# Up projection of the last four blocks by eleven half-width products in place of six full-width ones, with its sums spread over VectorE and GpSimd

## The chip, the cores and the metric

The kernel runs on one core of a Trainium2 chip. The metric is the device time of one execution in microseconds; the profile shows one execution, and the times are of executions of their own.

## The reference, cut to what matters

Two stages in float32. The first is a delta-rule attention with a state of 48 x 48 for each of 4 x 8 heads, over 768 positions; the second is an MLP with a hard-swish between its two products, over 3072 tokens (d_model 384, d_ff 2048).

```python
for t in range(S):                       # k_n: normalised keys
    y[:, :, t] = einsum('bhd,bhde->bhe', q[:, :, t], state)
    v_old = einsum('bhde,bhd->bhe', state, kt)
    state = state + bt[:, :, :, None] * einsum('bhd,bhe->bhde', kt, vt - v_old)
x = y.transpose(0, 2, 1, 3).reshape(B * S, H * D)          # 3072 x 384
h = x @ w_in                                               # w_in 384 x 2048
g = h * clip(h + 3.0, 0.0, 6.0) / 6.0
out = g @ w_out                                            # w_out 2048 x 384
```

## The kernel before, in words

**Tokens.** A token tile is 32 positions of all four batches, 128 rows; there are 24 (t = 0 to 23). Two token tiles make a block of the MLP (256 tokens, 12 blocks). Token tiles are also grouped for the attention's triangular inverse: group 0 is tile 0, then groups of four (1 to 4, 5 to 8, ... 17 to 20), the last, group 6, of three (21 to 23).

**Attention.** `prep(t)` normalises keys and scales them on GpSimd (L479, L457 the masks `mb`, L467 `bkb`), transposes keys and queries on TensorE (L495), copies them out with ScalarE (L503, the buffers `KQ`) and forms the score matrices (L516, evicted by VectorE at L527). `norms(g)` squares the keys (L385 on ScalarE in groups 0 to 3, L387 on GpSimd from group 4 on), reduces (L391) and takes roots. `inverse(g)` inverts the triangular matrices of a group by substitution on VectorE, 30 steps of a product (L728) and a difference (L733), with a transposition before and after (L447, L451). `chain(t)` carries the state: its products with keys and queries (`ks`, L775), R on VectorE (L788), the product with the inverse (`pz`, L796; Z on ScalarE, L882), the state's update (`su`, L893, L908), the output (`py`, L796; L812, L788, L831) and, last, the transposes `yt` (L841) that ScalarE copies into the block's `xT` (L845).

**MLP.** `up(blk)` forms, for each of 16 chunks of 128 hidden units, three matmuls of 256 columns (the three slices of d_model; L947) into a PSUM tile `ph`; ScalarE takes the relu (L955), VectorE the minimum and the product (L958) into the tiles `g`, two chunks in each. `down` (L987) is used for blocks 0 and 1. From block 2 on `down_by_seven` does the down projection by seven products of half size (Strassen-Winograd): its sums of `g` are in place on VectorE (L1038), its products have 192 columns (L1052), ScalarE copies them out (L1059), VectorE adds them up (L1062), and SP writes them to DRAM. In float32 every matmul stands in the trace as two records, each with its weight load (PEld).

**Order.** The program is scheduled by hand: each engine's queue holds its instructions in the order in which the code issues them. The text `ORDER` issues everything up to the start of token tile 5, word by word. From then on a loop takes each token tile in 15 steps, u = 0 to 14. At a step it issues, in this order: the step's entry in `plan` (pieces of `chain` and `prep`), key loads, one unit of the MLP (`take(units)`: one chunk of `up`, or half a product of `down_by_seven`), and two or three pieces of `fill` (the norms, then the substitution, of a coming group). `plan` puts the state products at u = 0, R at 1, y at 3, `pz` at 4, `su` and `py` at 8, the state's sum and y's at 9, and the transposes into `xT` at 11. A block's 16 units of `up` and 14 of `down_by_seven` make 30 units, two token tiles: `up` of block 8 starts at u = 12 of tile 17 and ends at u = 12 of tile 18, and so on; that of block 11 begins at u = 12 of tile 23 and has no attention beside it for the most part.

PSUM tiles `pt`, `ph`, `po`, `pz`, `py`, `yt` share four buffers. `needs(...)` only asserts at build time that something was issued before; real waits come from the reads and writes of the buffers.

Of the kernel before, what the change touches and what calls it, by code (L numbers as in the profile page):

```python
# [9 lines left out]
FP32 = mybir.dt.float32  # L10
# [28 lines left out]
k*2 v h4 i2*2 u rb i2 gb n9 i2 u i2 v i2 ru i2 gu i2 u ru i2*3 v q gu i2 c n9 u k i2 u i2 u ru gu  # L39
q ru i2 gu i2 k n9 v i2 u h4 y4 i2 v*2 i2 n9 u y4 i2 q u*2 i2 u n9 ru i2*3 q k gu q*2 i2 n9 q i2*3  # L40
n9 u k n9 q e i2*4 ru u gu y4 h4 e n9 u y4 k n9 k*2 i2 k*5 i2*2 k*3 ru k ru gu i2 u gu p9 u e i2 u
i2*5 e u i2*4
# [4 lines left out]
def kernel(  # L47
# [65 lines left out]
    NKB, NQB, NBKB, NLB, NKQ = 2, 4, 8, 8, 7  # L113
    kbufs = [persist.tile([P, H, DP], FP32, name=f"kb{i}") for i in range(NKB)]
    qbufs = [persist.tile([P, H, DP], FP32, name=f"qb{i}") for i in range(NQB)]
    bkbufs = [persist.tile([P, H, DP], FP32, name=f"bkb{i}") for i in range(NBKB)]
# [46 lines left out]
    NVF = 3  # L163
# [213 lines left out]
    def norms(g, i0, n):  # L377

        kf = kfs[g]
        ss = small.tile([P, n, H], FP32, name="ss")  # L380
        for i in range(n):
            needs(("k", first(g) + i0 + i))
            sq = work.tile([P, H, D], FP32, name="sq", bufs=1)
            if g < 4:
                nc.scalar.activation(out=sq[:], in_=kf[:, i0 + i], func=ACTF.Square)  # L385
            else:
                nc.gpsimd.tensor_tensor(  # L387
                    out=sq[:], in0=kf[:, i0 + i], in1=kf[:, i0 + i], op=ALU.mult
                )
            yield 1  # L390
            nc.vector.tensor_reduce(out=ss[:, i, :], in_=sq[:], axis=AX.X, op=ALU.add)  # L391
            yield

        root = small.tile([P, n, H], FP32, name="root")
        nc.scalar.activation(out=root[:], in_=ss[:], func=ACTF.Sqrt, bias=tiny, scale=0.25)
        yield
        t = small.tile([P, n, H], FP32, name="nt")
        nc.vector.reciprocal(out=t[:], in_=root[:])
        yield
        nc.vector.scalar_tensor_tensor(  # L400
            out=t[:], in0=ss[:], scalar=0.25, in1=t[:], op0=ALU.mult, op1=ALU.mult
        )
        yield
        nc.vector.scalar_tensor_tensor(
            out=t[:], in0=t[:], scalar=1e-6, in1=root[:], op0=ALU.add, op1=ALU.add
        )
        yield
        inv = small.tile([P, n, H], FP32, name="inv", bufs=4)
        nc.vector.reciprocal(out=inv[:], in_=t[:])
        for i in range(n):  # L410
            invs[first(g) + i0 + i] = inv[:, i, :]
        yield
# [40 lines left out]
    def mask(t):  # L453
        mb = mbs[t] = work.tile([P, 2, NP, 2, C], FP32, name="mb")
        needs("beta")
        for e in range(2):
            nc.gpsimd.tensor_tensor(  # L457
                out=mb[:, e],
                in0=beta_tok[:, t, e:H:2].unsqueeze(2).unsqueeze(3).to_broadcast([P, NP, 2, C]),
                in1=mask2[:].unsqueeze(1).to_broadcast([P, NP, 2, C]),  # L460
                op=ALU.mult,
            )
        yield

    def scaled(t):
        needs(("kb", t), *pad(t), *([("bkb", t - NKB)] if t >= NKB else []))
        nc.gpsimd.tensor_tensor(  # L467
            out=bkbufs[t % NBKB][:, :, 0:D], in0=kbufs[t % NKB][:, :, 0:D],
# [69 lines left out]
    def product(t):  # L538
# [10 lines left out]
        ring("KQ", NKQ, ("x", t))  # L549
        VYTF = work.tile([P, 4, H * C], FP32, name="VY", tag="KQ", bufs=NKQ)  # L550
# [84 lines left out]
    def join(t):  # L635
# [7 lines left out]
        ring("KQ", NKQ, ("x", t))  # L643
        tiles = work.tile([P, 4, H, C], FP32, name="VY", tag="KQ", bufs=NKQ)
# [111 lines left out]
    def chain(t, whole=True):  # L756
# [8 lines left out]
        bkb = bkbufs[t % NBKB]  # L765
# [96 lines left out]
        else:  # L862
            needs("parity")
            Rt = work.tile([P, DM], FP32, name="R", bufs=1)
# [16 lines left out]
        Zt = work.tile([P, DM], FP32, name="Z", bufs=1)  # L881
# [20 lines left out]
        su = update() if t < N - 1 else []  # L902
        if whole:
            take(outs[t])
# [15 lines left out]

    gs, pos, evicts = {}, {}, []
# [13 lines left out]
    def up(blk, half_of=None):  # L935
# [5 lines left out]
        for f in range(NFC):  # L941
# [28 lines left out]
            yield  # L970

# [60 lines left out]
    def down_by_seven(blk):  # L1032
# [31 lines left out]
        settle()  # L1064
        product(4, A22, T4, 0)
        yield
        product(4, A22, T4, 1)
        copy(C21, 4, -1.0)
        yield
        product(2, A12, B21, 0)  # L1070
        yield
        product(2, A12, B21, 1)
        copy(C11, 2)
        sums(ALU.add, A22, A21, A22, lo)
        yield
        product(1, A11, B11, 0)
        sums(ALU.add, A22, A21, A22, hi)
        yield
        product(1, A11, B11, 1)
        copy(u, 1)  # L1080
# [36 lines left out]
    def mlp_units():  # L1117
# [3 lines left out]
        for f in range(0, NFC, WF):  # L1121
# [3 lines left out]
            for _ in range(WF):  # L1125
                next(u1)
                yield
        for blk in range(1, N // CB):
            if blk < FIRST:
                for c in range(CB):  # L1130
                    for f in range(0, NFC, WF):
                        if c == 0:
                            needs(*(("read", ("ph", blk, f + i, None)) for i in range(2)))
                        down(blk, c, f)
                        yield
            else:
                yield from down_by_seven(blk)
            if blk + 1 < N // CB:
                for n, _ in enumerate(up(blk + 1)):
# [21 lines left out]
    LA = 6  # L1161
    LE = 4
    LS = G0 + GS
# [85 lines left out]
    with tc.manual_schedule():  # L1249
# [12 lines left out]
        for t in range(LS, N):  # L1262
# [11 lines left out]
            if i == 2:  # L1274
# [11 lines left out]
                11: lambda: take(ch),  # L1286
                13: lambda: take(later),
# [6 lines left out]
            for u in range(NU):  # L1294
# [15 lines left out]
                take(fill, 2 + (u % 3 == 0))  # L1310
# [33 lines left out]
```

## Time and profile before

| What | us |
|---|---|
| median of 3 executions | 689.24 (689.07 to 690.17) |
| the profiled execution's own time | 688.24 |
| its span, from the first to the last instruction | 686.5 |
| TensorE (PE) matmul busy | 647.2 |
| VectorE (DVE) busy | 467.8 |
| ScalarE (ACT) busy | 238.9 |
| GpSimd (POOL) busy | 95.2 |
| granted TensorE clock, mean | 0.985 |

Rows of a group or of a timeline give: start, duration, engine, line, operation, what is written and read, shape, count, and in brackets the engine's idle time just before and what ended it. Matmuls are pipelined, so the duration of one (273 ns or more) is longer than its distance to the next; the distance is what a stream costs.

### The profile page before, as it was taken

To read this page: it belongs to the slowest core of one execution; us is meant where nothing else is said; L and a number is where in the kernel's file an instruction comes from. 1 tells how busy PE (TensorE), PEld (TensorE's weight loads), DVE (VectorE), ACT (ScalarE), POOL (GpSimd) and SP (SyncE) were. 2 spreads that over 40 slices of the span, in tenths; PEclk is the share of its full clock that TensorE was granted. 3 is DMA by queue.
4 is the path that set the end of the run, shared out by engine and by line. 5 is a ranking of instruction groups with operands and counts; after the bars stand their busy time and mean duration, and the time that the engine had idled before them with its cause. 6 is when DMAs were issued, how large, how long until landed. Compare 5 with 4: busy or idle time off the path is not lost.

```text
span 686.5 us, 25308 instructions
## 1 busy us (share of the span) xinstructions
PE 647.2 (94%) x11208; PEld 567.8 (83%) x11208; DVE 467.8 (68%) x1210; ACT 238.9 (35%) x476; POOL 95.2 (14%) x147
## 2 busy tenths in 40 slices
PE   2668989999999999999999999999999999999997
PEld 2458877776688988988988988988988989989997
DVE  5898776888746997846985745985546985445242
ACT  5995677421233232232232232232232132132220
POOL 6241022203521100400101302100000000000000
PEclk9977899999999999999999999999999999999999
DMA  7987125412041030031030030020020020000000
GB/s 197 246 199 189 37 66 139 82 24 47 15 79 30 2 68 6 2 78 29 3 64 9 3 71 2 2 61 1 3 48 2 2 48 2 25 3 1 25 0 24
DMA packets 88494, 33.20 MB, mean 48 GB/s; under 512 B 80160, under 2 KB 83232, under 8 KB 88384
## 3 DMA queue, kind: packets, MB, share of 16 engines
q1 hardware_dynamic: 88128, 31.29, 20.5%
q8 instruction: 88, 1.44, 0.9%
q10 hardware_dynamic: 256, 0.30, 0.2%
q14 instruction: 22, 0.18, 0.1%
HBM read 26.84 MB, written 4.72 MB: 46 GB/s over the span
## 4 chain that ended last, share of the span: by engine, by line
PE 73%; DVE 12%; DMA 7%; issue 3%; ACT 2%; SPq 1%; POOL 0%; DVEq 0%; ACTq 0%; POOLq 0%
PE ph L947 33%; PE po L1052 21%; PE po L987 4%; PE ks L775 3%; PE py L796 2%; PE su L893 2%; PE pz L796 2%; DVE g L1038 2%; DMA w_out<-in_moe_w_in_dram 2%; DVE pr L728 2%; DVE A L733 2%; PE sc L516 2%; PE pt L495 2%; DMA spare<-in_moe_w_in_dram 2%; DMA qb<-in_q_dram 1%
## 5 line engine op out<-in xcount | busy, mean ns | idle before, releaser
L947 PE MATMUL ph<-xT,w_in 128*128 128x256 f32 (+1 forms) x1248 | 271.3, 371 | 3.8 <-DVE g L958 2.3
L947 PEld LDWEIGHTS ph<-xT,w_in 128*128 128x128 f32 x1248 | 222.3, 194 | 33.1 <-DVE g L958 3.5
L955 ACT ACTIVATE g<-ph,halves 128x256 f32<-128x256 f32 (+1 forms) x208 | 94.4, 456 | 198.1 <-PE ph L947 196.5
L958 DVE SCALAR_TENSOR_TENSOR g<-g,ph 128x256 f32<-128x256 f32 (+1 forms) x208 | 81.7, 396 | 100.1 <-ACT g L955 99.9
L1052 PE MATMUL po<-w_out,g 128*128 128x192 f32 x640 | 113.3, 328 | 0.0
L1052 PEld LDWEIGHTS po<-w_out,g 128*128 128x128 f32 x640 | 103.9, 190 | 0.5
L1052 PE MATMUL po<-spare,g 128*128 128x192 f32 x480 | 84.8, 330 | 0.0
L1052 PEld LDWEIGHTS po<-spare,g 128*128 128x128 f32 x480 | 78.1, 190 | 1.8
L1038 DVE TENSOR_TENSOR g<-g 128x256 f32<-128x256 f32 x160 | 65.5, 463 | 0.5 <-PE po L1052 0.4
L733 DVE TENSOR_TENSOR A<-A,pr 128x30 f32<-128x30 f32 (+9 forms) x150 | 52.2, 348 | 3.4
L728 DVE TENSOR_TENSOR pr<-A 128x30 f32<-128x30 f32 (+9 forms) x150 | 51.1, 341 | 3.1
L334 ACT ACTIVATE spare<-spare,places 128x768 uint16<-128x768 uint16 (+1 forms) x56 | 52.4, 940 | 1.9 <-DMA spare<-in_moe_w_in_dram 1.0
L987 PE MATMUL po<-w_out,g 128*128 128x384 f32 x128 | 45.6, 493 | 0.0
L479 POOL TENSOR_TENSOR kb<-kf,inv 128x384 f32<-128x384 f32 x24 | 23.0, 958 | 155.2 <-PE pt L495 69.9
L457 POOL TENSOR_TENSOR mb<-beta_tok,mask 128x256 f32<-128x256 f32 x48 | 34.9, 748 | 66.6 <-DVE LB L527 66.5
L1059 ACT ACTIVATE o<-po 128x192 f32<-128x192 f32 x40 | 13.2, 330 | 88.1 <-PE po L1052 88.1
L503 ACT ACTIVATE KQ<-pt 128x512 f32<-128x512 f32 x48 | 28.1, 594 | 42.5 <-PE pt L495 42.0
L987 PEld LDWEIGHTS po<-w_out,g 128*128 128x128 f32 x128 | 23.2, 190 | 12.3
L775 PEld LDWEIGHTS ks<-state,KQ 64*64 64x64 f32 x1472 | 24.3, 136 | 10.2 <-issue 9.0
L845 ACT ACTIVATE xT<-yt 128x384 f32<-128x384 f32 x24 | 11.7, 486 | 57.3 <-PE yt L841 57.3
L775 PE MATMUL ks<-state,KQ 64*64 64x48 f32 x1472 | 27.7, 222 | 3.7 <-issue 2.9
L788 DVE SCALAR_TENSOR_TENSOR y<-ks,parity,y 128x192 f32<-128x192 f32 x46 | 17.0, 412 | 19.3 <-ACT y L812 19.3
(109 smaller groups left out, 594.8 us busy)
## 6 DMA issues: line engine op xcount, KB each, us to landing
kf<-in_k_dram SPq DMA_DIRECT2D x96, 48.0 KB, 2.7
qb<-in_q_dram SPq DMA_DIRECT2D x96, 48.0 KB, 3.0
vf<-in_v_dram SPq DMA_DIRECT2D x96, 48.0 KB, 2.2
out_dram<-o SPq DMA_DIRECT2D x92, 48.0 KB, 1.6
spare<-in_moe_w_in_dram SPq DMA_DIRECT2D x4, 768.0 KB, 6.5
w_out<-in_moe_w_in_dram SPq DMA_DIRECT2D x4, 768.0 KB, 5.9
w_out<-in_moe_w_out_dram SPq DMA_DIRECT2D x4, 768.0 KB, 6.5
spare<-in_moe_w_out_dram SPq DMA_DIRECT2D x4, 768.0 KB, 5.8
```

What stands on the lines that cost most here:

```text
L334: nc.scalar.activation(out=z, in_=z if n else d.bitcast(I16)[:, :, :, 3], func=func, bias=places[:, n : n + 1], scale=scale,)
L457: nc.gpsimd.tensor_tensor(out=mb[:, e], in0=beta_tok[:, t, e:H:2].unsqueeze(2).unsqueeze(3).to_broadcast([P, NP, 2, C]), in1=mask2[:].unsq ...
L503: nc.scalar.activation(out=KQ[:, :, 0:4:3, :] if j == 0 else KQ[:, :, 1:3, :], in_=pt[:].rearrange("q p (x y c) -> q (p x) y c", y=2, c=C) ...
L728: nc.vector.tensor_tensor(out=pv, in0=A[:, j + 1 :, j].unsqueeze(2).to_broadcast([n, w, j]), in1=A[:, j, 0:j].unsqueeze(1).to_broadcast([n ...
L733: nc.vector.tensor_tensor(out=A[:, j + 1 :, 0:j], in0=A[:, j + 1 :, 0:j], in1=pv, op=ALU.subtract)
L775: nc.tensor.matmul(ph[y][c, e, D * p : D * p + D], lhsT=KQ[r, p * B // 2 + b // 2, 2 * y : 2 * y + 2, :].rearrange("k y c -> k (y c)"), rh ...
L947: nc.tensor.matmul(ph[:, cols], lhsT=w_in[:, s, f * 128 : (f + 1) * 128], rhs=xT[:, s, cols], start=(s == 0), stop=(s == NKT - 1),)
L955: nc.scalar.activation(out=g, in_=ph, func=ACTF.Relu, bias=half, scale=1.0 / 6.0)
L958: nc.vector.scalar_tensor_tensor(out=g, in0=g, scalar=1.0, in1=ph, op0=ALU.min, op1=ALU.mult)
L987: nc.tensor.matmul(pos[c][:], lhsT=gs[blk, f // 2][:, f % 2, c * P : (c + 1) * P], rhs=w_out[:, f, :], start=(f == 0), stop=(f == NFC - 1),)
L1038: nc.vector.tensor_tensor(out=A(f, *out), in0=A(f, *a), in1=A(f, *b), op=op)
L1052: nc.tensor.matmul(ps[n][:], lhsT=A(f - f % 2, *a)[:, f % 2], rhs=b[:, f], start=(f == 0), stop=(f == HF - 1),)
```

## The change

For blocks 8 to 11 `up` is replaced by `up_by_eleven`. The first two slices of d_model and the two token tiles are treated as a 2 x 2 by 2 x 2 product, for a pair of hidden chunks j: seven products by Winograd's scheme in place of eight; the third slice adds four plain ones. Each of the eleven has 128 columns. `begin(j)` issues four of them, ScalarE copies their PSUM tile into `g`, and GpSimd makes three additions there; `end(j)` issues the other seven into the same PSUM tile, VectorE adds `g` to three quarters of it, ScalarE copies the fourth and takes the relu of all 512 elements into a scratch tile (the tile `o` of the output), and VectorE takes the minimum and the product. The order of units is begin 0, begin 1, end 0, begin 2, end 1, ... end 7: 16 units as before. The weights' sums (`weight_sums`) are made once on GpSimd, two operations a unit during the down projection of block 7. The sums of x (`token_sums`) are four operations on VectorE, issued at u = 12 of each odd token tile from 17 on.

While an `up_by_eleven` is being issued, `fill` gets one piece a step instead of two or three. The squares of groups 4 to 6 move from GpSimd to ScalarE. In `down_by_seven` product 1 comes first, before 4 and 2. To make room in SBUF for the sums, early buffers share their space (scratch of the first inverses, one mask, one `bkb`), the mask has one buffer instead of two after tile 8, Z takes R's buffer, V has two load buffers instead of three (four words `v` leave `ORDER`), `KQ` six instead of seven, `LB` seven instead of eight.

```diff
@@ ORDER: four words v less, the rest as it was
-    NKB, NQB, NBKB, NLB, NKQ = 2, 4, 8, 8, 7
+    LA, LE, LS = 6, 4, G0 + GS
+    NKB, NQB, NBKB, NLB, NKQ, NVY = 2, 4, 8, 7, 6, 2
+    NPR = NFC // 2
+    sums_in = persist.tile([P, 3, NPR, P], FP32, name="sums_in")
...
-    NVF = 3
+    NVF = 2
@@ norms
-            if g < 4:
-                nc.scalar.activation(out=sq[:], in_=kf[:, i0 + i], func=ACTF.Square)
-            else:
-                nc.gpsimd.tensor_tensor(
-                    out=sq[:], in0=kf[:, i0 + i], in1=kf[:, i0 + i], op=ALU.mult
-                )
+            nc.scalar.activation(out=sq[:], in_=kf[:, i0 + i], func=ACTF.Square)
...
@@ chain
-        Zt = work.tile([P, DM], FP32, name="Z", bufs=1)
+        Zt = Rt if t > 0 else work.tile([P, DM], FP32, name="R", bufs=1)
...
@@ new functions
+    T1x, T2x, T4x = (beta_tok[:, 8 * i : 8 * i + 8, 8:24] for i in range(3))
...
+    def weight_sums():
+        for j in range(0, NPR, 2):
+            r = slice(j, j + 2)
+            plus_minus(S1[:, r], W21[:, r], W22[:, r], ALU.add)
+            yield
+            plus_minus(S2[:, r], S1[:, r], W11[:, r], ALU.subtract)
+            yield
+            plus_minus(S4[:, r], W12[:, r], S2[:, r], ALU.subtract)
+            yield
+            plus_minus(W21[:, r], W11[:, r], W21[:, r], ALU.subtract)
+            yield
...
+    def token_sums(blk):
+        needs(("seam", blk * CB), ("seam", blk * CB + 1), ("up", blk - 1))
+        B11, B12, B21, B22, _, _ = (
+            x.rearrange("p (a b) -> p a b", b=16) for x in x_tiles(blk)
+        )
+        for out, a, b in ((T1x, B12, B11), (T2x, B22, T1x), (B12, B22, B12), (T4x, B21, T2x)):
+            nc.vector.tensor_tensor(out=out, in0=a, in1=b, op=ALU.subtract)
+        past.add(("sums", blk))
+
+    def up_by_eleven(blk):
+        needs(("sums", blk))
+        mode["slow"] = True
+        B11, T3x, B21, B22, B31, B32 = x_tiles(blk)
...
+        def begin(j):
+            key = ("ph", blk, "by", j)
+            ring("pm", NPM, key)
+            ph = phs[j] = psM.tile([128, 4, P], FP32, name="ph", tag="pm")
+            mm(ph, 0, W11[:, j], B11, start=True)
+            mm(ph, 1, S1[:, j], T1x)
+            mm(ph, 2, W21[:, j], T3x)
+            mm(ph, 3, S2[:, j], T2x)
...
+            nc.scalar.activation(out=gt, in_=ph[:], func=ACTF.Copy)
+            plus_minus(gt[:, 1], gt[:, 1], gt[:, 2], ALU.add)
+            plus_minus(gt[:, 2], gt[:, 0], gt[:, 1], ALU.add)
+            plus_minus(gt[:, 0], gt[:, 0], gt[:, 3], ALU.add)
+
+        def end(j):
+            ph = phs.pop(j)
+            mm(ph, 0, W12[:, j], B21)
+            mm(ph, 1, S4[:, j], B22)
+            mm(ph, 2, W22[:, j], T4x)
+            mm(ph, 0, W13[:, j], B31)
+            mm(ph, 1, W13[:, j], B32)
+            mm(ph, 2, W23[:, j], B31)
+            mm(ph, 3, W23[:, j], B32, stop=True)
...
+            nc.vector.tensor_tensor(out=gt[:, 3], in0=ph[:, 3], in1=gt[:, 2], op=ALU.add)
+            nc.vector.tensor_tensor(
+                out=gt[:, 1:3], in0=ph[:, 1:3],
+                in1=gt[:, 0].unsqueeze(1).to_broadcast([128, 2, P]), op=ALU.add,
+            )
+
+            def first():
+                nc.scalar.activation(out=gt[:, 0], in_=ph[:, 0], func=ACTF.Copy)
+                read(("ph", blk, "by", j))
+                ro = mlp.tile([128, CB, DM], FP32, name="o", bufs=1)
+                r = ro[:].rearrange("p c m -> p (c m)")[:, 0 : 2 * TB]
+                nc.scalar.activation(out=r, in_=g, func=ACTF.Relu, bias=half, scale=1.0 / 6.0)
+
+                def rest():
+                    nc.vector.scalar_tensor_tensor(
+                        out=g, in0=r, scalar=1.0, in1=g, op0=ALU.min, op1=ALU.mult
+                    )
...
+        for j in range(NPR):
+            end(j)
+            go(j - 1)
+            if j + 2 < NPR:
+                yield
+                begin(j + 2)
+                go(j)
+                yield
...
@@ down_by_seven: product 1 and its copy move to the front, sums keep their units
...
@@ the loop
+                12: lambda: token_sums(t // CB) if t % CB and t // CB >= UF else None,
...
-                take(fill, 2 + (u % 3 == 0))
+                take(fill, 1 if mode["slow"] else 2 + (u % 3 == 0))
```

(`UF` is 8; `go(j)` runs what `end(j)` left in hand, first `first`, at its next call `rest`.)

## The prediction

> **What bounds the kernel now.** I read the page first, then the windows by block, the chain of waits, the groups by shape and the timeline at the places that the change touches.
>
> ```profile
> span 686.5 us, 25308 instructions
> ...
> PE 647.2 (94%) x11208; PEld 567.8 (83%) x11208; DVE 467.8 (68%) x1210; ACT 238.9 (35%) x476; POOL 95.2 (14%) x147
> ```
>
> TensorE is busy for 94% of the span. The windows say where the rest is: in the first 200 us. In the stretch that the change rewrites it never pauses:
>
> ```profile
> 500.80:526.00 25.20, 25.20 (x357) 21.63 (x356) 11.88 (x27) 8.45 (x18) 0.00 (x0) 1.00 0.16 34
> ...
> 548.60:574.00 25.40, 25.40 (x358) 21.80 (x357) 19.50 (x56) 8.45 (x18) 0.00 (x0) 1.00 0.16 33
> ...
> 643.40:664.20 20.80, 20.80 (x98) 18.34 (x97) 6.69 (x16) 7.10 (x15) 0.00 (x0) 1.00 0.07 20
> ```
>
> These are the up projections of blocks 8, 9 and 11 (length, then PE, PEld, DVE, ACT, POOL busy, then the granted clock, 1.00). GpSimd does nothing there; VectorE is loaded only in block 9, where the last substitution runs. So what shortens TensorE's stream shortens the kernel, and any wait put into it lengthens the kernel. The end of the chain of waits prices the stream:
>
> ```profile
> 643.64 20.72 PE ph L947 x96
> 664.36 18.21 PE po L1052 x112
> ```
>
> A product stands in the trace as two records. 20.72 / 96 = 215.8 ns for a record with 256 moving columns.
>
> **Part 1: eleven products of 128 columns for six of 256 (the saving).** Now a pair of hidden chunks takes 6 products x 2 records x 215.8 = 2,590 ns. After, it takes 11 x 2 = 22 records of 128 columns. Block 0 already runs this line at 128 columns, with a new weight each time:
>
> ```profile
> 58.26 2.31 PE L947 MATMUL ph<-xT,w_in 128*128 128x128 f32 x18 [0.27 <-DVE g L958]
> 60.88 4.29 PE L947 MATMUL ph<-xT,w_in 128*128 128x128 f32 x36 [0.30 <-DVE g L958]
> ```
>
> The second row less the 0.27 of its last record and the 213 ns between its first two starts is 3.81 us for 34 steps: 112 ns, and read start by start they are 111 to 113. The transposes, also 128 columns, lie 109 ns apart. I take 111.7 ns, the row with this line's operands: 22 x 111.7 = 2,457 ns, 133 ns less a pair, and 8 pairs x 4 blocks x 133 ns = **-4.3 us** (at 109 ns: -6.1). It is a third of what eleven for twelve sounds like: 111.7 is more than half of 215.8.
>
> [...]
>
> **Part 2: x's sums (a new wait in TensorE's stream).** `token_sums` is issued at step 12 of each odd token tile. Step 11 issues the transposes, ScalarE's copy into xT and the last half of product 3, with VectorE's addition that closes C12; the eleven begin at step 12. So the sums stand in VectorE's queue behind an addition that waits for TensorE's last matmul of the block before:
>
> ```profile
> 499.25 0.49 PE L841 MATMUL yt<-ident,y 128*128 128x128 f32 x3
> ...
> 499.58 1.47 PE L1052 MATMUL po<-w_out,g 128*128 128x192 f32 x8
> ...
> 499.78 0.49 ACT L845 ACTIVATE xT<-yt 128x384 f32<-128x384 f32 x1 [5.72 <-PE yt L841]
> ...
> 500.88 2.32 PE L947 MATMUL ph<-xT,w_in 128*128 128x256 f32 x10
> 501.08 0.35 DVE L1062 TENSOR_TENSOR o<-u,po 128x192 f32<-128x192 f32 x1 [1.06 <-PE po L1052]
> ```
>
> Call 500.88 zero. The addition starts at 0.20. Additions of 192 elements are 0.35 long; an independent one starts 0.28 after its predecessor, a dependent one 0.39. The substitution's rows at 130 elements are 0.30 long. So T1 runs 0.48 to 0.78, T2 (which reads T1) to 1.11, T3 to about 1.33. TensorE's second product needs T1, the third T3, the fourth T2. T3 is seen at about 1.40; two products and the 0.1 us by which the record after a wait comes late make 1.95 instead of 0.89: a wait of 1.06, say 1.1 us. In blocks 8, 10 and 11 VectorE has nothing else. At block 9 the profile shows two substitution steps (0.43 each) between that addition and step 12, and the addition 0.28 later: T1 then starts 1.14 later, 2.2 us of wait. Together 3 x 1.1 + 2.2 = **+5.5 us**. Below, if T1 alone counts, 0.5 less a block: +3.5; above, if the first product too waits for T3, +7.
>
> **Part 3: what hangs on each pair.** ScalarE: a copy of 512 elements (0.59, row of KQ L503), one of 128 (0.28), a relu of 512 (0.47 for 256, so about 0.69): 1.56 us for 0.95 now. VectorE: 0.28 + 0.42 out of PSUM and 0.69 for the 512 product: 1.39 for 0.84. GpSimd: three additions of 128; its rows are 0.83 at 384 and 0.60 to 0.71 at 256, so 0.37 to 0.57 each, 1.1 to 1.7. All are under the pair's 2.46 us. What TensorE needs of them is ScalarE's copy before `end(j)`. It finishes about 0.85 us after `begin(j)`; in between TensorE runs `end(j-1)` and `begin(j+1)`, 22 records, 2.46 us: 1.6 us of cover. If that is gone it is rival B. GpSimd slows VectorE where both its inputs lie in SBUF:
>
> ```profile
> 435.32 0.76 DVE L1038 TENSOR_TENSOR g<-g 128x256 f32<-128x256 f32 x2
> ...
> 437.51 1.42 POOL L457 TENSOR_TENSOR mb<-beta_tok,mask 128x256 f32<-128x256 f32 x2 [6.45 <-DVE LB L527]
> 437.61 1.59 DVE L1038 TENSOR_TENSOR g<-g 128x256 f32<-128x256 f32 x2
> ```
>
> Two sums take 1.59 beside GpSimd, 0.76 alone. Of a pair only the 512 product is open to that: up to 1.1 us, VectorE 1.8 of 2.46. With the state chain (3.8 us a token tile, 0.4 a pair) it fits; in block 9 one substitution step a unit adds 0.7 a pair, and it just closes. I take nothing here.
>
> **Part 4: the weight sums.** 16 additions of 256 on GpSimd, about 0.7 each, 11 us, once, behind the last mask, from about 466 us on. VectorE's two-input work of that time (the end of a substitution, then the 16 sums of block 7) can lose up to 0.4 an operation; products follow those sums with a unit or more to spare. Between 0 and +2; I take **+0.3**, near the end of no loss, for that distance.
>
> **Part 5: squares on ScalarE.** They matter once, at token tile 5:
>
> ```profile
> 168.59 0.55 DVE L391 TENSOR_REDUCE ss<-sq 128x8 f32<-128x384 f32 x1 [0.94 <-POOL sq L387]
> ...
> 170.09 0.55 DVE L391 TENSOR_REDUCE ss<-sq 128x8 f32<-128x384 f32 x1 [0.94 <-POOL sq L387]
> ...
> 174.57 0.86 PE L516 MATMUL sc<-KQ 64*32 64x64 f32 x64 [1.15 <-ACT y L812]
> ```
>
> VectorE waits for two squares of 0.83 and only then computes R; TensorE stands 1.2 us at L516 behind it. ScalarE's square is 0.51 (L385): about 0.3 less each, **-0.7 us** (-1.2 to 0, since ScalarE's KQ copy now queues behind them).
>
> **Part 6: the rest.** The thinned substitution of group 6 ended at 565 us, inside block 9. Counting steps (8 in tile 18, 31 in 19, 19 in 20), 4 of its 62 now fall to the start of tile 21: 2.7 us of VectorE ahead of R, whose product comes 7.3 us after the state's matmuls (479.27 to 486.62 in tile 17). Product 1 first lets the late last pairs finish under 3.9 us of matmuls; their chain (additions, pair 6's product, relu, pair 7's product at 0.7 each, and hops) is about 3.1. Single buffers (mask, Z in R's, fewer V and KQ) add waits for readers that ended a unit or a tile earlier: SP's V loads now wait for R two tiles back, with 25 us to their use. Together **+0.2** (0 to +1).
>
> **Sum.** -4.3 + 5.5 + 0.3 - 0.7 + 0.2 = +1.0. The profiled execution took 688.24 us (1.74 around the span); the median is 689.24, so I forecast 689.2 + 1.0 = 690.2 us. A difference under 0.2%, 1.4 us, can't be told from none here.
>
> **Rivals.** *Forecast: the wait eats the saving.* 688.7 to 691.7, chance 0.45 (0.26 of it within 0.2%). *A: the sums are in time (faster).* If VectorE hands T1 to T3 over before the second and third products, only block 9's extra 1.1 is left: -3.4, 685.8. It decides once the four waits total under 3.1 us. For it: xT is ready 0.6 us before zero, and 109 ns records would add 1.8. Against: the closing addition stands first in the queue and can't start before 0.20. Chance 0.27 (684.5 to 687.8). *B: pairs wait on ScalarE (slower).* Its copy for pair j+3 stands behind the relu of pair j, which waits for VectorE's additions and, through the one scratch tile, for the product of pair j-1. Once VectorE is over 1.6 us late, all of the excess is TensorE's: 0.15 us on each of 32 pairs is +4.8, 695.0. For it: VectorE's load in block 9; against: 6.69 us of work in block 11's 20.8. Chance 0.22 (691.7 to 698). *C: 128 columns aren't that cheap.* T1, T2 and T4 are read in runs of 16 elements, which no row shows; at twice the time, 3 x 2 x 112 ns x 32 = +21 us, 711. Chance 0.06.
>
> So faster 0.27, same 0.26, slower 0.47. The range 685.0 to 695.0 leaves out some 0.07 of A below and 0.12 of B and C above.
>
> **What would show it.** Right: records 111 to 113 ns apart in the up stages of blocks 8 to 11, 19.7 us without waits in the last; a TensorE gap before the second and third products, released by VectorE, near 1 us and twice that at block 9; no ScalarE release inside. Wrong: no such gap (A), repeated gaps at `end` (B), wider steps (C), or gaps in the first 450 us.

## The result, and the profile after

The changed kernel takes 693.49 us (median of 20 executions) against 690.12 for the kernel before on the same chip: ratio 1.0048, interval 1.0031 to 1.0066, or 3.4 us slower. Single executions of either kernel differ by several microseconds (those of before range from 687.5 to 693.5), and the traces differ most in the first 165 us; so a trace is used below to say where time goes, and medians to say how much. The profiled execution of after took 689.89 us, that of before 688.24.

The page of after, its span and its busy times, and two of its groups (busy time, mean ns of one, idle time before):

```profile
span 687.8 us, 26297 instructions
...
PE 645.7 (94%) x11528; PEld 575.8 (84%) x11528; DVE 485.7 (71%) x1258; ACT 262.9 (38%) x519; POOL 140.3 (20%) x248
...
L1005 POOL TENSOR_TENSOR g<-g 128x128 f32<-128x128 f32 x96 | 43.8, 458 | 145.7 <-ACT g L1053 140.6
L1039 PE MATMUL ph<-xT,w_in 128*128 128x128 f32 x448 | 70.0, 280 | 0.3
```

GpSimd has gained 45 us of work, and an addition of 128 elements costs it 458 ns, inside the 0.37 to 0.57 that the prediction gave it. TensorE's busy time is only 1.5 us less. The end of the chain of waits has the new stage of block 11 (start, length, what):

```profile
646.24 19.50 PE ph L1039 x172
665.74 18.22 PE po L1196 x112
```

These are 172 records of 128 columns without a pause, mostly 111 to 112 ns apart start by start. The pause is ahead of them. The timeline of after where block 11's up projection begins:

```profile
644.81 0.38 PE L1039 MATMUL ph<-xT,w_in 128*128 128x128 f32 x2
645.01 0.35 DVE L1206 TENSOR_TENSOR o<-u,po 128x192 f32<-128x192 f32 x1 [1.06 <-PE po L1196]
645.28 0.29 DVE L1029 TENSOR_TENSOR beta_tok<-xT 128x128 f32<-128x128 f32 x1
645.60 0.29 DVE L1029 TENSOR_TENSOR beta_tok<-xT,beta_tok 128x128 f32<-128x128 f32 x1
645.62 0.49 PE L1039 MATMUL ph<-beta_tok,sums_in 128*128 128x128 f32 x2 [0.43 <-DVE beta_tok L1029]
```

The first product starts at 644.81, the closing addition 0.20 later, T1 0.47 later, and the second product, which reads T1, waits for it. Read start by start over the first eight records, this pause and the next (for T3) cost 0.59 + 0.10 + 0.30 + 0.07 = 1.06 us. It is the same in blocks 8 and 10.

Block 9 is another matter. The timeline of after, VectorE and TensorE (some rows left out):

```profile
545.44 0.35 DVE L1206 TENSOR_TENSOR u<-u,po 128x192 f32<-128x192 f32 x1
545.89 0.36 DVE L1206 TENSOR_TENSOR o<-o,u 128x192 f32<-128x192 f32 x1
546.12 0.38 PE L1039 MATMUL ph<-xT,w_in 128*128 128x128 f32 x2
546.28 0.36 DVE L1206 TENSOR_TENSOR o<-o 128x192 f32<-128x192 f32 x1
546.56 0.40 DVE L751 TENSOR_TENSOR A<-A,pr 128x240 f32<-128x240 f32 x1
...
548.17 0.35 DVE L1206 TENSOR_TENSOR o<-u,po 128x192 f32<-128x192 f32 x1
548.44 0.40 DVE L751 TENSOR_TENSOR A<-A,pr 128x238 f32<-128x238 f32 x1
548.87 0.40 DVE L746 TENSOR_TENSOR pr<-A 128x234 f32<-128x234 f32 x1
549.19 0.28 DVE L1029 TENSOR_TENSOR beta_tok<-xT 128x128 f32<-128x128 f32 x1
...
549.53 0.79 PE L1039 MATMUL ph<-beta_tok,sums_in 128*128 128x128 f32 x2 [3.02 <-DVE beta_tok L1029]
```

VectorE is not idle for more than 0.1 us anywhere here. It is behind: the closing additions start only at 545.44, and the last of them, which in block 11 comes 0.20 after the first product, comes 2.05 after it. TensorE stands idle for 3.02 us. And the two records at the end of this fence take 0.79, not 0.49. The windows around the pause (length, then PE, PEld, DVE, ACT and POOL busy, the granted clock, DMA):

```profile
546.10:549.50 3.40, 0.41 (x4) 0.21 (x2) 3.13 (x10) 0.00 (x0) 0.00 (x0) 0.99 0.08 21
549.50:552.80 3.30, 3.27 (x14) 3.18 (x15) 1.41 (x5) 0.60 (x1) 0.67 (x2) 0.50 0.36 98
552.80:556.00 3.20, 3.20 (x83) 3.03 (x82) 1.24 (x4) 0.60 (x1) 2.07 (x5) 1.00 0.36 66
```

For 3.3 us after the pause the granted clock is 0.50, and the records come 213 ns apart: there are twelve of them, which costs 1.2 us. With the wait (3.19 + 0.26 + 0.13 and what follows it) block 9 pays 4.9 us.

**Where the time went, by the two traces.** The table gives after minus before at the same matmuls (the state products of tiles 6 and 17, and the end).

| Stretch | After minus before at its end | What happened in it |
|---|---|---|
| up to tile 6 | -4.76 | start and early tiles; varies between executions |
| tiles 6 to 17 | -2.91 | +1.85: the old blocks, where nothing of the new stage runs |
| tile 17 to the end | +1.33 | +4.24: saving -4.0, waits and clock 3 x 1.06 + 4.9 = +8.1, 0.1 left |

The saving of 4.0 is 4 x 1.0, from block 11 of the first experiment, which has no wait (19.73 us for 176 records, 20.72 before).

### The profile page after: what moved, and what is told of

It reads as the page before. It is cut to its first block, busy times and chain, and to the rows that moved or that the text cites. A ratio compares the mean times of both kernels' runs of the same rounds, so it can differ in the third digit from the quotient of the medians.

```text
span 687.8 us, 26297 instructions
## 1 busy us (share of the span) xinstructions
PE 645.7 (94%) x11528; PEld 575.8 (84%) x11528; DVE 485.7 (71%) x1258; ACT 262.9 (38%) x519; POOL 140.3 (20%) x248
## 4 chain that ended last, share of the span: by engine, by line
PE 73%; DVE 19%; ACT 3%; issue 2%; DMA 1%; SPq 1%; DVEq 0%; ACTq 0%
PE ph L968 22%; PE po L1196 19%; PE ph L1039 12%; PE po L1131 4%; DVE g L1182 3%; DVE A L751 3%; DVE pr L746 3%; PE ks L793 3%; PE pz L814 2%; PE py L814 2%; PE su L912 2%; PE pt L513 2%; PE sc L534 2%; ACT spare L348 2%; DVE o L1206 1%
## 5 line engine op out<-in xcount | busy, mean ns | idle before, releaser
L968 PE MATMUL ph<-xT,w_in 128*128 128x256 f32 (+1 forms) x864 | 184.2, 366 | 5.3 <-DVE g L979 2.9
L968 PEld LDWEIGHTS ph<-xT,w_in 128*128 128x128 f32 x864 | 149.9, 195 | 24.9 <-DVE g L979 3.9
L976 ACT ACTIVATE g<-ph,halves 128x256 f32<-128x256 f32 (+1 forms) x144 | 64.2, 450 | 131.9 <-PE ph L968 131.8
L1196 PEld LDWEIGHTS po<-w_out,g 128*128 128x128 f32 x640 | 104.5, 190 | 0.3
L979 DVE SCALAR_TENSOR_TENSOR g<-g,ph 128x256 f32<-128x256 f32 (+1 forms) x144 | 55.0, 386 | 51.6 <-ACT g L976 51.3
L473 POOL TENSOR_TENSOR mb<-beta_tok,mask 128x256 f32<-128x256 f32 x38 | 25.9, 704 | 236.7 <-DVE LB L545 236.7
L1005 POOL TENSOR_TENSOR g<-g 128x128 f32<-128x128 f32 x96 | 43.8, 458 | 145.7 <-ACT g L1053 140.6
L1039 PE MATMUL ph<-xT,w_in 128*128 128x128 f32 x448 | 70.0, 280 | 0.3
L1039 PEld LDWEIGHTS ph<-xT,w_in 128*128 128x128 f32 x448 | 59.7, 194 | 1.5 <-issue 0.8
L1053 ACT ACTIVATE g<-ph 128x512 f32<-128x512 f32 x32 | 19.1, 597 | 50.5 <-PE ph L1039 50.5
L1069 DVE TENSOR_TENSOR g<-ph,g 128x128 f32<-128x128 f32 x32 | 9.2, 289 | 36.1 <-POOL g L1005 22.4
```

The source lines that it names most:

```text
L968: nc.tensor.matmul(ph[:, cols], lhsT=w_in[:, s, f * 128 : (f + 1) * 128], rhs=xT[:, s, cols], start=(s == 0), stop=(s == NKT - 1),)
L976: nc.scalar.activation(out=g, in_=ph, func=ACTF.Relu, bias=half, scale=1.0 / 6.0)
L979: nc.vector.scalar_tensor_tensor(out=g, in0=g, scalar=1.0, in1=ph, op0=ALU.min, op1=ALU.mult)
L1005: nc.gpsimd.tensor_tensor(out=out, in0=a, in1=b, op=op)
L1039: nc.tensor.matmul(ph[:, n], lhsT=w, rhs=x, start=start, stop=stop, skip_group_check=True)
L1196: nc.tensor.matmul(ps[n][:], lhsT=A(f - f % 2, *a)[:, f % 2], rhs=b[:, f], start=(f == 0), stop=(f == HF - 1),)
```

## The experiments

The theory after the result: the waits for x's sums, VectorE's lateness at block 9 and the halved clock behind it eat the saving; something in the old blocks adds 1.85. The rivals: the records themselves or the pairs cost more than they seem to; the slow stretch in block 9 is memory traffic or GpSimd, not the clock; the 1.85 come from the squares, the order of the products, or the buffers.

**1. The sums ahead of the queue.** `token_sums` is issued at step 11, right after the transposes into xT and ahead of the last half of product 3 and its closing additions.

```diff
-                11: lambda: take(ch),
-                12: lambda: token_sums(t // CB) if t % CB and t // CB >= UF else None,
+                11: lambda: (take(ch), token_sums(t // CB) if t % CB and t // CB >= UF else None),
```

> The four sums of x are issued at step 11, right behind the copy into xT and ahead of the closing additions of the block before. Theory (VectorE's queue order makes the wait): in blocks 8, 10 and 11 the wait inside the first eleven products, 0.9 us each in the changed kernel, falls under 0.2 us; at block 9, where VectorE is late by itself, it falls from 3.7 to about 1.7 us, and with the pause short the records behind it are 112 ns apart again, not 213 (another 1.4 us). Together about 5.5 us less than the changed kernel: 0.992 of it, 0.997 of the kernel before. Rival (the wait is only moved: the closing addition and with it the output's DMA and the scratch tile come later, and TensorE waits for ScalarE instead): no more than 1 us less than the changed kernel, with gaps at the seventh to tenth unit of each up stage.

Measured: 686.36 us, 0.9946 of before (0.9922 to 0.9969); 7 us less than after. In blocks 8, 10 and 11 no wait is left. The timeline of this kernel at block 8:

```profile
500.31 0.29 DVE L1029 TENSOR_TENSOR beta_tok<-xT 128x128 f32<-128x128 f32 x1 [0.94 <-ACT xT L863]
...
500.89 0.38 PE L1039 MATMUL ph<-xT,w_in 128*128 128x128 f32 x2
...
501.11 0.39 PE L1039 MATMUL ph<-beta_tok,sums_in 128*128 128x128 f32 x2
```

T1 starts 0.58 ahead of the first product; the second product follows without a pause. In block 9 VectorE is still late and 1.3 us of wait remain, but the clock stays up:

```profile
549.53 0.49 PE L1039 MATMUL ph<-beta_tok,sums_in 128*128 128x128 f32 x2 [1.15 <-DVE beta_tok L1029]
...
549.50:552.80 3.30, 3.14 (x25) 2.98 (x26) 3.08 (x9) 1.19 (x2) 1.10 (x3) 1.00 0.14 38
```

From tile 17 to the end this trace is 6.3 us better than after's: 3 x 1.06, and in block 9 a cost of 1.8 for 4.9. The wait was the cost, and a version faster than both kernels is one moved line away.

**2. Everything but the new stage.** The up projection of before in all blocks, all else as in after.

```diff
-    UF = 8
+    UF = N
```

> All of the change but its core: no block uses the eleven products, so no weight sums, no sums of x and no thinned substitution; squares on ScalarE, product 1 first and the smaller buffers stay. Theory (the loss lies in the up stages of blocks 8 to 11): 0.999 of the kernel before, 0.3 to 0.7 us less, from the squares at token tile 5, and the changed kernel's extra time gone; from token tile 6 to the end the same within 0.5 us as before. Rival (buffers, mask and load order cost time before tile 17): 1.002 or more of the kernel before, with more gaps at tiles 8, 12 and 16.

Measured: 688.67 us, 0.9976 (0.9951 to 1.0000). By its trace it also loses 1.84 us between tiles 6 and 17, where the expectation had allowed 0.5, and nothing behind tile 17 (-0.2). So the 1.85 come from the accompanying edits and not from the new stage, and what after loses behind tile 17 is the new stage's own.

**3. The sums twelve times.** T1 is formed twelve times over, so that each pause grows beyond 4 us, block 11's too, where VectorE has little else to do.

```diff
-        for out, a, b in ((T1x, B12, B11), (T2x, B22, T1x), (B12, B22, B12), (T4x, B21, T2x)):
+        for out, a, b in ((T1x, B12, B11),) * 12 + ((T2x, B22, T1x), (B12, B22, B12), (T4x, B21, T2x)):
```

> The first sum of x is formed twelve times over, so that VectorE hands it over some 3 us later at each of blocks 8, 10 and 11 (the result is the same). Theory (a pause of about 3 us halves TensorE's granted clock for some 3.3 us): the wait there grows from 0.6 to 3 to 4 us, and behind it the records lie 213 ns apart for 3 us or more, at each block whose pause passes about 3 us: 1.4 us lost on top of each wait, 13 to 17 us in all over the changed kernel. Rival (the wide steps after block 9's wait come from the output DMAs or from GpSimd's additions beside it): 112 ns steps right after the longer waits, 9 to 12 us in all.

Measured: 713.39 us in one execution. The repeats cost 0.32 us each, so the waits became 4.26, 6.77, 4.17 and 4.17 us (first two records start to start, less 0.11; TensorE's idle times in them are 4.09, 6.60, 4.01 and 4.00). Windows behind them, one for each of blocks 8 to 10 and two for block 11:

```profile
505.00:508.40 3.40, 3.31 (x16) 3.17 (x17) 0.61 (x3) 0.73 (x2) 1.01 (x3) 0.62 0.24 42
560.80:564.20 3.40, 3.35 (x15) 3.27 (x16) 1.41 (x5) 0.60 (x1) 0.75 (x2) 0.50 0.33 52
...
614.90:618.30 3.40, 3.33 (x15) 3.22 (x16) 0.71 (x4) 0.60 (x1) 0.73 (x2) 0.52 0.27 49
666.80:670.20 3.40, 3.33 (x15) 3.24 (x16) 0.71 (x4) 0.60 (x1) 0.73 (x2) 0.50 0.01 2
670.20:673.00 2.80, 2.80 (x15) 2.80 (x15) 0.00 (x0) 0.60 (x1) 2.00 (x5) 0.50 0.02 6
```

The clock falls behind each of the four pauses, to 0.62, 0.50, 0.52 and 0.50 in the window that follows it, in block 11 with DMA at 0.01, VectorE busy for 0.71 of 3.40 us and GpSimd for 0.75. That rules out memory traffic and a busy VectorE as the cause, and GpSimd is busy for longer in block 11 of after, 1.78 of 3.40 us from 646.20 on, where no record is slow. The slow records go with the pause. Against after's profiled execution it is 23.5 us: 14.4 in the waits, about 6.7 in slow records (they last 3.2, 5.1, 2.4 and 5.1 us, half of it lost, less the 1.2 of after), and 2.6 ahead of tile 5, where traces differ anyway. It is more than the expected 13 to 17 because of these early 2.6, and because each repeat was longer and two stretches were 5.1 us, not 3.3.

**4. The squares alone.** The kernel of before with the squares of all groups on ScalarE.

```diff
-            if g < 4:
-                nc.scalar.activation(out=sq[:], in_=kf[:, i0 + i], func=ACTF.Square)
-            else:
-                nc.gpsimd.tensor_tensor(
-                    out=sq[:], in0=kf[:, i0 + i], in1=kf[:, i0 + i], op=ALU.mult
-                )
+            nc.scalar.activation(out=sq[:], in_=kf[:, i0 + i], func=ACTF.Square)
```

> The kernel before with the squares of all groups on ScalarE, nothing else changed. Theory (part 5 of the prediction): the reductions at token tile 5 no longer wait 0.94 us for GpSimd, and TensorE's stall of 1.2 us at the score product of that tile falls by 0.5 to 0.7 us; from there on no difference. Rival (ScalarE's copies queue behind squares that wait for VectorE): the stall stays at 1 us or more, or moves to the copies of KQ. As the early part also differs from run to run, the wait is read, not the time.

Measured: 689.93 us in one execution. The timeline of this kernel at token tile 5:

```profile
170.67 0.55 DVE L386 TENSOR_REDUCE ss<-sq 128x8 f32<-128x384 f32 x1 [0.59 <-ACT sq L384]
...
171.81 0.55 DVE L386 TENSOR_REDUCE ss<-sq 128x8 f32<-128x384 f32 x1 [0.59 <-ACT sq L384]
...
175.96 0.86 PE L511 MATMUL sc<-KQ 64*32 64x64 f32 x64 [1.44 <-ACT y L807]
```

VectorE's two waits fell from 0.94 to 0.59, as the prediction said; TensorE's stall behind them did not fall with them, it is 1.44 for 1.15. Over all traces this stall is 1.1 to 1.2 where the squares are on GpSimd, 1.4 where they are on ScalarE with the early buffers of before or nearly so (here and in experiments 10 and 11), and 0.6 where they are on ScalarE with the early buffers of after. Neither edit alone shortens it. From tile 6 to 17 this kernel loses 0.07 in all (0.43 at tile 12, regained at tile 16 but for 0.07), so the squares aren't the 1.85.

**5. The old order of products.** Experiment 1 with product 1 ahead of 4 and 2 only in blocks 8 to 11.

```diff
+        if blk >= UF:
             product(1, A11, B11, 0)
...
+        else:
+            product(4, A22, T4, 0)
+            yield
+            product(4, A22, T4, 1)
...
```

> The sums of x first (step 11), and product 1 first only in blocks 8 to 11; blocks 2 to 7 keep the order of the kernel before (4, 2, 1). From token tile 6 to 17 the changed kernel and the one without the eleven lose 1.85 us against the kernel before, in gaps at the first units of the up stages of tiles 8, 12 and 16 and at two transposes. Theory (product order: the in-place sums of A22 now wait for product 4 just before them and VectorE falls behind): the loss falls to 0.3 us or less; 1.5 us less than with the sums first alone, 0.992 of the kernel before. Rival (the smaller buffers, above all the single mask, make VectorE or GpSimd late): the loss stays 1.85 us, 0.9945 of the kernel before.

Measured: 685.99 us, 0.9934 (0.9911 to 0.9957), not distinguishable from experiment 1. Tiles 6 to 17 still lose 1.77 us by its trace, so the order of products isn't it either.

**6. The substitution paused ahead of block 9's sums.** Experiment 5, and at steps 9 to 11 of token tile 19 `fill` gets no piece; one piece more each third step of the new stage makes up for it.

```diff
-                if i == 1 == ready[0] and 5 < u < 12:
+                if i == 1 == ready[0] and 5 < u < 12 or i == 2 and t // CB >= UF and 8 < u < 12:
...
-                take(fill, 1 if mode["slow"] else 2 + (u % 3 == 0))
+                take(fill, (1 if mode["slow"] else 2) + (u % 3 == 0))
```

> As the one before, and the substitution pauses at steps 9 to 11 of token tile 19, so that VectorE is not late for block 9's sums; inside the up stages it takes two pieces instead of one at every third step, which makes up for the seven that are left out. Theory (block 9's wait is VectorE's own lateness): the wait of 1.3 us there falls under 0.3 us, no gap elsewhere; 1 us less than without the pause, 0.990 to 0.991 of the kernel before. Rival (the steps that move make VectorE late inside block 9 or before R of tile 21): gaps of 0.5 us or more there, and no gain.

Measured: 686.89 us, 0.9933 (0.9908 to 0.9959); the same as experiment 5. The timeline at block 9 shows the wait gone:

```profile
548.80 0.29 DVE L1029 TENSOR_TENSOR beta_tok<-xT 128x128 f32<-128x128 f32 x1
...
549.38 0.38 PE L1039 MATMUL ph<-xT,w_in 128*128 128x128 f32 x2
...
549.60 0.39 PE L1039 MATMUL ph<-beta_tok,sums_in 128*128 128x128 f32 x2
```

From tile 19's state product to tile 20's this trace gains 1.8 us on experiment 5's, and it loses 1.0 of them again by the end. What was put off shows at 569 us, where TensorE loses 0.36 to a wait for VectorE, and at 583 us, where 1.97 us of the substitution's transposition now stand ahead of R and TensorE loses 0.3 and 0.2 in two steps. More than half of the gain was given back: VectorE's queue was merely rearranged.

**7. The buffers alone.** The kernel of before with the change's buffers (shared early space, one mask, `bkb`, Z in R, V, KQ, LB): experiment 2 with the old order of products and the squares on GpSimd.

> The kernel before with the change's buffers alone: scratch of the first inverses in its own space and no longer in the ring of KQ, KQ six, LB seven, V two (with the four words less in the order), one mask after tile 8, Z in R's place; products, their order and squares as before. All four kernels with these buffers reached the state products of token tile 5 at 161.0 to 163.9 us, the two without at 165.2 and 166.0. Theory (the first inverses no longer wait for slots of KQ): tile 5 at 161 to 164 us, 0.995 to 0.997 of the kernel before, and from tile 6 to 17 no loss if product order made it, 1.85 us if the buffers did. Rival (chance of the run, or the order of loads): tile 5 at 165 to 166 us, no difference in time.

Measured: 689.00 us, 0.9972 (0.9953 to 0.9992). By its trace 1.42 of the 1.85 are there. The median is nevertheless lower than before's, by 1.9 us by the ratio, so the buffers must gain some 3 us elsewhere, in the first tiles by exclusion; the one trace shows no such gain (it reaches tile 5 at 165.1 us, 0.1 ahead of before, and not at the expected 161 to 164).

**8 and 9. Which buffer.** The kernel of before with one mask buffer from token tile 10 on (8), and with seven of the eight `bkb` from tile 8 on (9).

```diff
+        late = t >= LS + LE
+        if late:
+            needs(("L", t - 1))
-        mb = mbs[t] = work.tile([P, 2, NP, 2, C], FP32, name="mb")
+        mb = mbs[t] = mb_pair[0 if late else t % 2]
```

> The kernel of before with one mask buffer from token tile 10 on, for two; nothing else. Question: which of the tighter buffers moves GpSimd's product for kb beside VectorE's last sums of the out projection (1.04 us for 0.42 there, tiles 8, 12 and 16), and so loses 1.4 of the 1.85 us of tiles 6 to 17. If the mask is it: the sums of tiles 12 and 16 have one of 1.0 us, and TensorE loses 0.3 to 0.6 us at each against before; tile 8 is as before. If it is the ring of the beta-scaled keys: nothing changes from before, tile 6 to tile 17 within 0.2 us. If neither alone: the same as before here and in the next run.

```diff
+    def bkb_of(t):
+        return bkbufs[t if t < NBKB else 1 + (t - 1) % (NBKB - 1)]
...
+        if t >= NBKB:
+            needs(("su", t - NBKB + 1))
```

> The kernel of before with seven buffers of beta-scaled keys from token tile 8 on, for eight; nothing else. If this ring is what moves GpSimd's work: at tiles 8, 12 and 16 the product for bkb waits for the update product (su) seven tiles back, the product for kb behind it falls on VectorE's sums (one of 1.0 us), and tile 6 to tile 17 is 1 to 1.5 us longer than before. If it is the mask: within 0.2 us of before.

Measured: 689.21 and 692.18 us, one execution each. Between tiles 6 and 17 the mask's kernel loses 1.72 us by its trace, the other 0.26. So one mask buffer alone is enough for the loss, and one `bkb` less is not. GpSimd's timeline in before, late in tile 11:

```profile
334.33 1.41 POOL L457 TENSOR_TENSOR mb<-beta_tok,mask 128x256 f32<-128x256 f32 x2 [6.45 <-DVE LB L527]
335.70 1.00 POOL L387 TENSOR_TENSOR sq<-kf 128x384 f32<-128x384 f32 x1
```

and with one mask:

```profile
333.95 1.37 POOL L461 TENSOR_TENSOR mb<-beta_tok,mask 128x256 f32<-128x256 f32 x2 [23.35 <-DVE LB L531]
335.28 1.01 POOL L471 TENSOR_TENSOR bkb<-kb,beta_tok 128x384 f32<-128x384 f32 x1
336.25 0.96 POOL L483 TENSOR_TENSOR kb<-kf,inv 128x384 f32<-128x384 f32 x1
```

The mask of the next tile now has to wait for the last reader of the one before, and the two products behind it in GpSimd's queue come in one burst with it, 3.3 us for 2.4. VectorE is in the last sums of a block and a substitution then, all of them operations with both inputs in SBUF, which GpSimd slows here (Part 3's two sums 1.59 us for 0.76; the relu's product L958, with one input in PSUM, takes 0.42 alone and 0.42 beside `kb` at 301.45 us of before). One more of them is hit: late in tile 7, beside `kb`, a row of the substitution takes 0.84 for the 0.33 of before. In after `bkb` also waits for the product `su` (3.77 us), since its ring is smaller, and `bkb` and `kb` come as a pair some 4 us behind the mask. They still fall on the same sums: one that takes 0.42 alone takes 1.05 (late in tile 7 of after, two of them 2.02 for 0.75):

```profile
231.73 0.88 POOL L485 TENSOR_TENSOR bkb<-kb,beta_tok 128x384 f32<-128x384 f32 x1 [3.77 <-PE su L912]
231.84 2.02 DVE L1182 TENSOR_TENSOR g<-g 128x256 f32<-128x256 f32 x2
...
232.58 1.01 POOL L497 TENSOR_TENSOR kb<-kf,inv 128x384 f32<-128x384 f32 x1
```

VectorE has no room to catch up (in after it is busy for 15.17 of the next 15.90 us), R and the relu's product come that much later, and TensorE waits 0.5 to 0.7 us more at each of tiles 8, 12 and 16. My expectation that tile 8 would be as before was wrong: tile 10's mask is already written there.

**10 and 11. The spare buffers kept to tile 16.** The second mask and the eighth `bkb` lie where the weight sums go, which are written from 463 us on. Experiments 5 and 6 with both in use until tile 16.

```diff
-        early = t < LS + LE
-        if t > 1 or not early:
+        early = t < 16
+        if t > 1:
...
-        return bkbufs[t if t < NBKB else 1 + (t - 1) % (NBKB - 1)]
+        return bkbufs[t % NBKB if t < 16 else 1 + (t - 2) % (NBKB - 1)]
...
-            needs(("su", t - NBKB + 1))
+            needs(("su", t - NBKB + (t >= 16)))
```

> The version x5_old_order (sums first, the product order of before in blocks 2 to 7) with the spare mask buffer and the spare key buffer, which lie in the space of the weight sums, kept in use until token tile 16 instead of tile 8 or 10. If the early hand-over of these buffers is what costs: tiles 8 and 12 lose nothing against before, tile 16 still does, and the whole is about 1.2 us under x5_old_order, near 684.8 us, 0.992 of before. If the loss has another cause (R's and Z's common buffer, V's, the KQ ring): no change from x5_old_order, 686.

> The same change of buffers on x6_paused (the substitution paused ahead of block 9's sums). If buffers and pause each hold: the wait of 1.3 us in block 9 is gone as well, and what of it later stages give back is as in x6_paused; 684 to 685.5 us. If the buffers are not it: as x6_paused, 686 to 687.

Measured: 686.88 us, 0.9945 (0.9924 to 0.9967), and 686.61 us, 0.9943 (0.9921 to 0.9966). By the traces tile 8 loses nothing any more, tiles 12 and 16 still do, and 1.21 of 1.77 us are lost between tiles 6 and 17 instead of all. This agrees with the mask as the cause, and shows why the change of buffers fell short: GpSimd runs ahead, and the mask of tile 16, the first to wait for its predecessor, is already next in its queue in tile 9 (written at 284 us), so that tile 12 meets one buffer again. The gain of 0.6 us is below what the medians can tell; the expected 1.2 did not come, and the five versions with the sums first (1, 5, 6, 10, 11) are one result: 0.5 to 0.7% under before.

## Why the prediction was right in its time and where its sum was not

The forecast was that the wait for x's sums eats the saving, 690.2 us from 689.24, or +1.0; measured is +3.4, against a before of 690.12. Mechanism and sign of the likeliest case hold: the wait exists, and it exceeds the saving. Two terms were far too small (block 9's wait and Part 6), one cost and one gain were missing (the clock, and the early tiles).

The time itself was met with luck. 693.5 us lies outside 688.7 to 691.7, the bounds of the forecast's own case, and inside those of rival B, whose mechanism did not occur. It stays within 685.0 to 695.0 only because an early gain of some 2.7 us, which no term held, hides that the other terms together came to +6.1 and not to the +1.7 that they were given; without it the time would have been near 696.

| Term | Predicted | Measured, and by what |
|---|---|---|
| Part 1, the products | -4.3 | -4.0: block 11 without a wait takes 19.73 us for 20.72 (experiment 1) |
| Part 2, the wait in blocks 8, 10, 11 | +1.1 each | +1.06 each; gone in experiment 1 |
| Part 2, the wait in block 9 | +2.2 | +3.7 |
| the clock after it | not foreseen | +1.2; shown in experiment 3 |
| Part 3, per pair | 0 | 0: no ScalarE release inside the stages |
| Part 4, the weight sums | +0.3 | 0: from tile 16 to tile 17, where they begin, after loses 0.30 against before, as experiments 2 and 8 do without them |
| Part 5, the squares | -0.7 | from tile 5 to 6, -0.5 in after, +0.6 with the squares alone; the stall is 0.5 shorter and 0.3 longer |
| Part 6, buffers and order | +0.2 | +1.85 in tiles 6 to 17; one mask buffer alone makes 1.7 |
| the rest, by difference from +3.4 | | -2.7, Part 5 within it, ahead of tile 6 |

**Part 1** was right to read the price of a narrow record from block 0's rows: 111.7 ns there, and the records are at 111 to 112.

**Part 2** is right in blocks 8, 10 and 11 down to the order of VectorE's queue. In block 9 the step that failed is "the profile shows two substitution steps between that addition and step 12, and the addition 0.28 later". That was read in the trace of before, where VectorE is already busy for most of tile 19. The same window of before and, in the second fence, of after (length, then PE, PEld and, third, DVE busy):

```profile
526.00:542.00 16.00, 16.00 (x265) 15.18 (x267) 14.48 (x46) 3.08 (x8) 0.00 (x0) 1.00 0.01 1
```

```profile
526.00:542.00 16.00, 16.00 (x331) 15.31 (x330) 15.38 (x50) 2.59 (x7) 0.00 (x0) 1.00 0.02 4
```

VectorE has 14.48 of 16.0 in before and 15.38 in after: there was no room. T1 starts 3.07 us after the first product, for 1.62 in the prediction. The chain of block 8's last pairs, which follows `end(7)`, ends only at 526.3 us, and the substitution stands behind it. Its thinning, which Part 6 counted and Part 2 did not, works the same way: between the state products of tiles 18 and 19 VectorE does 9 of its operations in before and none in after, in the next tile 31 and 37. The additions before the closing one were late as well, so the queue's delay was not the number of steps between two instructions but everything VectorE owed by then, 2 us. A queue as busy as this one (14.48 of 16.0 us in before) has to be counted from the last moment at which it was empty.

**The clock** was the missing term. In the prediction a wait cost its own length. Here a pause of 3.02 us cost 1.2 more, one of 1.15 us in experiment 1 nothing. Behind the first the granted clock was 0.50 for 3.3 us, behind the second 1.00; behind the 4.00 to 6.60 us of experiment 3 the windows read 0.50 to 0.62.

The length of one pause alone does not decide the clock, as the early part of the traces shows. In before the clock falls to 0.50 at 68.4 us, and in the 3.4 us ahead of that TensorE was busy for 1.86 and never idle for more than 1.05 at a stretch:

```profile
64.90:68.30 3.40, 1.86 (x133) 1.58 (x132) 2.46 (x9) 1.44 (x4) 0.00 (x0) 1.00 0.72 183
68.40:75.10 6.70, 5.30 (x122) 4.55 (x124) 3.52 (x10) 3.23 (x7) 0.00 (x0) 0.50 0.49 102
```

No run sets the pause between 1.15 and 3.02 us, so what one of such a length does in a dense stretch was not shown.

**Part 6** failed at "single buffers add waits for readers that ended a unit or a tile earlier". That was read for the mask as for Z and V: the wait itself costs nothing. What it does is move the products that stand behind it in GpSimd's queue, and Part 3 had the price of that in its own fence, two sums at 1.59 beside GpSimd and 0.76 alone. It was asked only for the new stage's products. The sums in the old blocks are where it fell.

**Part 5 and the early tiles.** From tile 5 to tile 6, where the squares matter, after gains 0.5 us by its trace; the squares alone lose 0.6, so the gain needs the early buffers too. Ahead of that after is 4.3 us in front at tile 5 in the profiled executions, but that place varies by itself. After and experiments 1, 2, 3, 5, 6 and 7 issue the same instructions on the four engines up to 156 us, and they reach tile 5 at 161.0, 163.9, 161.0, 163.5, 164.8, 165.4 and 165.1 us; before and experiments 4, 8 and 9, with the early buffers of before, at 165.2, 166.0, 164.2 and 168.9. The clock varies with it: between the state products of tiles 1 and 2 it stands at 0.50 for 13.7 of 33.7 us in before and for 6.8 of 29.3 in after. The early gain of about 3 us follows from the medians (2.5 to 4.2 by difference in after and in experiments 1, 2, 5, 6, 7, 10 and 11) and isn't located; it stays open which of the buffers makes it, and how much of it is the clock.

**The rivals.** A, the sums in time, is what experiment 1 builds: A put it at 685.8, and 686.4 was measured, but with block 9's wait, the old blocks' loss and the early gain in it, so that the agreement is in part chance. B, pairs that wait on ScalarE, and C, wider records, are refuted by the trace: no release by ScalarE within the four stages, and distances of 111 to 113 ns but for the pauses, the slow stretch and a few records 0.1 late.

## What to carry to other kernels

When an edit makes TensorE wait for an engine at a seam, look at what stands in that engine's queue ahead of the awaited instruction; issuing four small sums one step earlier was worth 7 us here, more than the saving of the whole scheme. Price a wait not only by its length but by whether the clock falls behind it (1.2 us more behind 3.02 us here), and price a smaller buffer by which later instructions its wait moves and what they then run beside. A late queue is not mended by moving its work: of the 1.8 us that a pause in the substitution won, more than half came back as waits within two tiles.

## What the runs showed of the hardware that was not expected

In a dense stretch, a pause of TensorE of 3.02 us (after, block 9) was followed by a granted clock of 0.50 for 3.3 us, and pauses of 4.00 to 6.60 us (experiment 3) by 0.50 to 0.62 in windows of 3.4 us; fp32 records of 128 columns came 213 ns apart for 111 there, during 2.4 to 5.1 us. After a pause of 1.15 us (experiment 1) the clock was 1.00 and they did not. In the early tiles of before the clock fell without such a pause (TensorE busy for 1.86 of 3.40 us, idle for at most 1.05 at a stretch). VectorE's operations with both inputs in SBUF, 0.33 to 0.42 us alone, took 0.84 to 1.05 beside a GpSimd product of 384 elements (late in tile 7 of experiment 8 and of after), and that product 1.01 for 0.83; the relu's product, with one input in PSUM, took 0.42 either way (L958 in before).
